# A complex-decay linear attention with two MLP layers: state factor written in one piece, its small transfers asked for where X and Y are formed, prologue and step pieces in a new order

## The chip, the cores and the metric

The kernel runs on one core of a Trainium2 chip. A time is the device time of one execution in microseconds (us), and the metric is the median over executions. The engines are PE (TensorE, matmuls, with PEld for its weight loads), DVE (VectorE), ACT (ScalarE), POOL (GpSimd) and SP (SyncE), which in this kernel asks for every transfer.

## The reference

Three parts follow one another. A linear attention with a complex decay per token and channel runs over 4 batches, 8 heads, 768 tokens and a head size of 48; its output, as 3072 tokens of 384 values, goes through two MLP layers with 2048 inner channels, the first with h cos(h), the second with ELU.

```python
mag = np.sqrt(a_re * a_re + a_im * a_im)
scale = np.minimum(mag, 0.999) / (mag + 1e-06)
a_re_n, a_im_n = (a_re * scale, a_im * scale)
for t in range(S):
    ar, ai = (a_re_n[:, :, t, :, None], a_im_n[:, :, t, :, None])
    new_re = ar * S_re - ai * S_im
    new_im = ar * S_im + ai * S_re
    kv = np.einsum('bhd,bhe->bhde', k[:, :, t], v[:, :, t])
    S_re, S_im = (new_re + kv, new_im)
    y[:, :, t] = np.einsum('bhd,bhde->bhe', q[:, :, t], S_re)
...
h = x @ w_in                                   # layer 1
g = h * np.cos(h)
x = g @ w_out
h = x @ w_in                                   # layer 2
g = np.where(h > 0.0, h, np.exp(np.minimum(h, 0.0)) - 1.0)
return g @ w_out
```

## The kernel before

**Attention.** The 768 tokens of a batch are cut into 6 chunks of 128. A step is one chunk c of one batch b; there are 24, in the order (0,0), (0,1), (0,2), (0,3), (1,0) and so on, so the same batch comes again four steps later. A step loads arai (a_re and a_im side by side), qk and v; forms the logarithm L of the decay's size and its angle th (`a1_pre`, `a1_ln`, `a1_lam`, `a1_th`); sums both over the chunk with a matmul by a triangle (`p_tl`, `p_tf`, L245, L247); and gets E and En, the exponentials of plus and minus the summed logarithm (`a2_exp`, ACT L262, L263), and the phase r (`a2_ph`, L279, L280), whose sine and cosine are cs (`a2_trig`, L291, L292). `a2_mag` (L299) multiplies E into q and En into k. `a2_xy` (L306) forms X from q and Y from k, each 128x768. `b_tr` (PE L314) transposes X and Y in two groups of four heads, `b_ev` evacuates the results as XT (ACT L323) and YT (L325), `b_sc` (PE L332) multiplies them to scores and masks these as AT (DVE L335), `b_y` (L357, L366) forms the outputs, and `b_ds` (PE L376, DVE L382 or L384) updates the state S of the batch by Y, v and the factor R. `x_split` (ACT L408, DVE L409) writes a step's output as two parts, xh and xl, of which the MLP takes three products for exactness. For steps 0 to 2 all these tiles lie in `scr`, memory that the weights take over later.

**What goes through DRAM.** Two rows of a step are wanted in another shape or by another step. R is E's last row, 384 values, wanted as 96x8 (twice the same 48x8): `a2_exp` writes it to r_d (L267) and fetches it twice (L270). The last row of r is the phase that the batch carries on: `a2_ph` writes it to f_d (L282), and four steps later `a1_carry` reads it into a row of the tile w (L237), which DVE adds to th (L228).

**MLP.** A block is three steps, 384 tokens. A unit is 128 of the 2048 inner channels for one block in one layer: nine matmuls into `work` (L504), a chain on ACT, DVE and POOL (for layer 1 ACT L558, DVE L559, ACT L575, DVE L576, then gh on ACT L175 and gl on POOL L176), and nine matmuls into `acc` (L610). Layer 1 runs eight units of block 0, eight of block 1, the other eight of each, then blocks 2 to 7 with 16 units each; layer 2 follows. Weights come as 64-bit floats in 16 tiles a layer: a load `raw` (L451), a decode `dec` on DVE and ACT (L466 or L469, L470, L471, L473), and a split into two parts (DVE L487 or ACT L489, then L491). Those of layer 2 are decoded during layer 1, written to w2f and read back.

**What sets the order.** The string PRO lists the prologue: tokens as `exp:1` are the part of that name for that step, and R, D and P the next weight's load, decode and split. From there on the list SLOT cuts each step into eight pieces, and a rule (`goal`) deals the pieces out between the MLP units so that a block's three steps are done before its units. J2 and J2E say how many blocks before the end of layer 1 the second layer's decodes begin and over how long they spread, WS the spread of splits. A scheduler then orders PE, DVE, POOL and SP by priorities; ACT keeps the order in which the code is written. YTA is the number of steps whose YT is evacuated on ACT, YG the number whose Y is formed on DVE and not POOL, ED the number of layer-1 weights whose first decode and split operations run on DVE and not ACT. Each engine runs its instructions in order, and SP waits at each transfer for what that transfer needs.

Of the kernel before, what the change touches and what calls it, by code (L numbers as in the profile page):

```python
# [11 lines left out]
F32 = mybir.dt.float32  # L12
# [22 lines left out]
YTA, RHP, CARP = 0, 0, 0  # L35
NDF = 24
MG, YG = 5, 3
KEEP = (1,)
J2, J2E = 4, 4
# [6 lines left out]
PRO = ('Q:2 L:1 L:0 V:1 L:2 V:0 R Q:0 R pre:1 Q:1 pre:0 ln:0 D pre:2 ln:1 ln:2 lam:0 lam:1 lam:2 tl:0 tl:1 tl:2 exp:0 exp:1 th:0 th:2 P L:3 exp:2 R mag:1 R tf:0 th:1 ph:0 tf:1 ph:1 mag:0 trig:0 xy:0 D tr0:0 tf:2 trig:1 tr1:0 ph:2 ev0:0 ds:0 ev1:0 xy:1 sc0:0 tr0:1 sc1:0 y0:0 tr1:1 trig:2 mag:2 y1:0 ev0:1 xy:2 xs:0 sc0:1 ev1:1 V:2 sc1:1 y0:1 y1:1 tr0:2 tr1:2 ds:1 ev0:2 ev1:2 D D sc1:2 pre:3 P sc0:2 xs:1 y0:2 ln:3 lam:3 y1:2 ds:2 xs:2 D th:3 P tf:3')  # L46
SLOT = ['xs:-1 pre:2', 'tl:1 tf:1 exp:1 ph:1 tr0 ev0 ln:2', 'tr1 sc0 y0 lam:2 ev1 trig:1', 'sl:2 L:3 sc1 mag:1',
        'ca:2', '', 'th:2', 'Q:2 sp:2 y1 xy:1 ds V:2']
NRAW, NDEC, NL, NTH = 3, 2, 1, 1
FA, NXB, ED, P0 = 8, 3, 5, 1  # L50
WS = 18
# [6 lines left out]
def tile_kernel(ctx, tc, q, k, v, a_re, a_im, w_in, w_out, w2_in, w2_out, ari, qk, vp, w1p, w2p, out):  # L58
# [23 lines left out]
    r_d = dram.tile([NS, D, H], F32, name="r_d")  # L82
# [173 lines left out]
    def a2_exp(i):  # L256
        s = st[i]
        c, b = steps[i]
        E = buf(i, "E")
        En = buf(i, "En")  # L260
        table(LN_SET)
        nc.scalar.activation(out=E, in_=s["Lp"][:, 0:HD], func=AF.Exp, scale=0.5)  # L262
        nc.scalar.activation(out=En, in_=s["Lp"][:, 0:HD], func=AF.Exp, scale=-0.5)  # L263
        s["E"], s["En"] = E, En
        if c < NCH - 1:
            R = ap.tile([D2, H], F32, name="R", bufs=2)
            nc.sync.dma_start(out=r_d[i:i + 1].rearrange("o d h -> o h d"),  # L267
                              in_=E[P - 1:P, :].rearrange("p (h d) -> p h d", h=H))
            for x in range(2):
                nc.sync.dma_start(out=R[x * D:(x + 1) * D, :], in_=r_d[i])  # L270
            s["R"] = R

    def a2_ph(i):
# [7 lines left out]
        if c < NCH - 1:  # L281
            nc.sync.dma_start(out=f_d[i:i + 1, :], in_=r[P - 1:P, :])  # L282
# [18 lines left out]
    def a2_xy(i):  # L301
        s = st[i]
        for nm, m, eng in (("X", "q", nc.vector), ("Y", "k", nc.vector if i < YG else nc.gpsimd)):
# [24 lines left out]
    def b_sc(i, g):  # L328
        s = st[i]
        ps = work()  # L330
# [38 lines left out]
    def b_ds(i):  # L369
        s = st[i]  # L370
        c, b = steps[i]
        if c == NCH - 1:
            return
        ps = work()
# [549 lines left out]
```

## Time and profile before

| | us |
|---|---|
| median of 3 executions | 1122.48 (1118.74 to 1123.85) |
| profiled execution | 1120.67 |
| its span | 1119.0 (1.7 lie outside) |
| PE busy in the span | 1048.4 (94%) |
| DVE busy | 636.9 (57%) |
| ACT busy | 744.4 (67%) |
| POOL busy | 493.6 (44%) |

The profile of one execution lists for each engine how long it worked; for a stretch, how much of it; for a group of equal operations, how many there were and how long one took; and the chain of waits, which is followed back from the last instruction of a stretch to what released each one. PE is idle for 70.6 us of the span in all. Of those, 26.8 lie before 60 us, 12.3 in 60 to 90, 8.7 in 90 to 150 and 6.9 in 150 to 240. The granted clock of PE is 1.00 at full speed (2.4 GHz) and 0.50 at half.

### The profile page before, as it was taken

The page shows a single profiled execution, that of the slowest core. Times are in us where ns is not written, and L with a number is a line of the kernel's source. Part 1 is how long each engine was busy: PE and PEld are TensorE (multiplying, and loading weights), DVE is VectorE, ACT ScalarE, POOL GpSimd, SP SyncE. Part 2 cuts the span into 40 slices and gives each one's busy share as a digit, 9 for nine tenths or more (in the row PEclk, how much of TensorE's full clock was granted, in tenths as well). Part 3 has the DMA queues.
Part 4 walks back from the last instruction along what each step waited for, and adds up shares of the span by engine and source line. Part 5 has one row for each costly group of instructions (what it writes and reads, how often), then busy time and mean ns, then how long its engine had stood idle before and what let it go on. Part 6 is the DMA issues. An engine that isn't in the chain of part 4 may idle for free.

```text
span 1119.0 us, 19085 instructions
## 1 busy us (share of the span) xinstructions
PE 1048.4 (94%) x7202; PEld 985.3 (88%) x7202; DVE 636.9 (57%) x1076; ACT 744.4 (67%) x1452; POOL 493.6 (44%) x422
## 2 busy tenths in 40 slices
PE   2877798999999999989999999999999999999997
PEld 0655686899999989989998799989999999999997
DVE  6885789855565646766876455554333333333332
ACT  6466677774776756766876356776666666666664
POOL 1023545454554534644754136783434343443432
PEclk9996899999999989989999999999999999999999
DMA  7744723321131351253443154541000010100000
GB/s 203 117 93 112 114 94 106 94 66 45 49 48 51 48 129 60 82 169 129 149 145 122 55 165 156 184 146 52 22 22 22 23 43 1 43 1 22 1 22 25
DMA packets 45397, 90.33 MB, mean 81 GB/s; under 512 B 14025, under 2 KB 24817, under 8 KB 45297
## 3 DMA queue, kind: packets, MB, share of 16 engines
q1 hardware_dynamic: 45296, 89.04, 28.7%
q8 instruction: 58, 0.95, 0.4%
q14 instruction: 43, 0.34, 0.1%
HBM read 72.05 MB, written 16.97 MB: 80 GB/s over the span
## 4 chain that ended last, share of the span: by engine, by line
PE 75%; ACT 8%; DVE 7%; DMA 4%; issue 3%; POOL 2%; SPq 0%; POOLq 0%; DVEq 0%; ACTq 0%
PE work L504 33%; PE acc L610 24%; PE work L610 6%; PE work L314 3%; ACT L94 3%; PE work L357 2%; PE work L332 2%; PE work L366 2%; DMA w<-f_d 1%; PE work L376 1%; DVE dec L471 1%; DVE AT L335 1%; DMA r_d<-E 1%; ACT XT L323 1%; PE work L245 1%
## 5 line engine op out<-in xcount | busy, mean ns | idle before, releaser
L504 PE MATMUL work<-xh,wt 128*128 128x384 f32 x1536 | 446.8, 346 | 4.7 <-POOL wt L491 2.3
L176 POOL TENSOR_TENSOR gl<-t,gh 128x384 fp32r<-128x384 f32 x256 | 277.6, 1086 | 375.5 <-ACT gh L175 147.2
L504 PEld LDWEIGHTS work<-xh,wt 128*128 128x128 f32 x1536 | 282.7, 191 | 15.2 <-issue 6.5
L504 PE MATMUL work<-xl,wt 128*128 128x384 f32 x768 | 223.5, 339 | 0.1
L610 PE MATMUL acc<-gh,wt 128*128 128x384 f32 x768 | 194.7, 346 | 1.5 <-ACT gh L175 1.1
L175 ACT CAST gh<-t 128x384 fp32r<-128x384 f32 x256 | 130.0, 508 | 98.0 <-PE acc L610 68.1
L565 DVE SCALAR_TENSOR_TENSOR t<-e,t 128x384 f32<-128x384 f32 x128 | 75.6, 591 | 204.9 <-ACT t L564 145.9
L610 PE MATMUL acc<-wt,gh 128*128 128x384 f32 x512 | 158.0, 334 | 0.0
L504 PEld LDWEIGHTS work<-xl,wt 128*128 128x128 f32 x768 | 142.0, 190 | 1.4 <-issue 1.0
L610 PEld LDWEIGHTS acc<-gh,wt 128*128 128x128 f32 x768 | 136.4, 190 | 7.2 <-ACT gh L175 3.3
L558 ACT ACTIVATE t<-work 128x384 int32<-128x384 f32 x128 | 61.7, 482 | 67.3 <-PE work L504 58.3
L610 PE MATMUL acc<-gl,wt 128*128 128x384 f32 x384 | 102.9, 338 | 2.0 <-POOL gl L176 1.8
L576 DVE TENSOR_TENSOR t<-work,t 128x384 f32<-128x384 f32 x128 | 70.6, 552 | 57.4 <-ACT t L575 57.2
L610 PEld LDWEIGHTS acc<-wt,gh 128*128 128x128 f32 x512 | 95.0, 188 | 0.0
L562 ACT ACTIVATE t<-work 128x384 f32<-128x384 f32 x128 | 62.8, 490 | 41.2 <-PE work L504 31.4
L559 DVE SCALAR_TENSOR_TENSOR t<-t,work 128x384 f32<-128x384 int32 x128 | 69.8, 546 | 30.8 <-ACT t L558 29.9
L306 POOL TENSOR_TENSOR Y<-cs,qk 128x768 f32<-128x768 f32 x21 | 51.2, 2440 | 78.6 <-ACT cs L292 35.9
L610 PE MATMUL work<-wt,gh 128*128 128x384 f32 x256 | 85.5, 334 | 0.0
L575 ACT ACTIVATE t<-t,hpi 128x384 f32<-128x384 f32 x128 | 78.9, 617 | 3.6 <-DVE t L559 3.5
L610 PE MATMUL acc<-wt,gl 128*128 128x384 f32 x256 | 76.2, 334 | 0.0
L578 DVE SCALAR_TENSOR_TENSOR t<-work,t 128x384 f32<-128x384 f32 x128 | 71.3, 557 | 4.3
L610 PEld LDWEIGHTS acc<-gl,wt 128*128 128x128 f32 x384 | 69.1, 188 | 4.3 <-POOL gl L176 3.6
(135 smaller groups left out, 1697.9 us busy)
## 6 DMA issues: line engine op xcount, KB each, us to landing
raw<-in_w1p_dram SPq DMA_DIRECT2D x16, 768.0 KB
raw<-in_w2p_dram SPq DMA_DIRECT2D x16, 768.0 KB
chk<-in_ari_dram SPq DMA_DIRECT2D x24, 384.0 KB
arai<-in_ari_dram SPq DMA_DIRECT2D x21, 384.0 KB
qk<-in_qk_dram SPq DMA_DIRECT2D x21, 384.0 KB
v<-in_vp_dram SPq DMA_DIRECT2D x24, 256.0 KB
w2f<-dec SPq DMA_DIRECT2D x16, 384.0 KB
raw<-w2f SPq DMA_DIRECT2D x16, 384.0 KB
```

Source lines behind the costliest of these rows:

```text
L175: nc.scalar.copy(out=hi, in_=x)
L176: nc.gpsimd.tensor_tensor(out=lo, in0=x, in1=hi.bitcast(F32), op=ALU.subtract)
L306: eng.tensor_tensor(out=t, in0=s["cs"], in1=mm.to_broadcast([P, H, 2, D]), op=ALU.mult)
L504: nc.tensor.matmul(out=out_ps, lhsT=a, rhs=b_, start=m == 0, stop=m == n - 1)
L558: nc.scalar.activation(out=ki, in_=h, func=AF.Copy, scale=1.0 / TWO_PI, bias=0.25)
L559: nc.vector.scalar_tensor_tensor(out=t, in0=ki, scalar=-TWO_PI, in1=h, op0=ALU.mult, op1=ALU.add)
L562: nc.scalar.activation(out=t, in_=h, func=AF.Relu, scale=-1.0)
L565: nc.vector.scalar_tensor_tensor(out=t, in0=e, scalar=1.0, in1=t, op0=ALU.add, op1=ALU.mult)
L575: nc.scalar.activation(out=t, in_=t, func=AF.Sin, bias=hpi)
L576: nc.vector.tensor_tensor(out=t, in0=h, in1=t, op=ALU.mult)
L578: nc.vector.scalar_tensor_tensor(out=t, in0=h, scalar=0.0, in1=t, op0=ALU.max, op1=ALU.add)
L610: nc.tensor.matmul(out=o, lhsT=a, rhs=b_, start=(l, j, ff) in first and x == 0, stop=(l, j, ff) in last and x == 2)
```

## The change

- r_d holds [step, head, channel] and not [step, channel, head]. The write of E's last row becomes one contiguous row of 384 values; each of the two fetches into the 48x8 halves of R now picks single values.
- The two writes (r_d and f_d) move from `a2_exp` and `a2_ph` into a function `send`, called at the start of `a2_xy`. The fetch moves into `fetch`, called at the first scores of a step (`b_sc`) or, if that has not been, in `b_ds`.
- YT of steps 0 to 3 is evacuated on ACT (YTA 0 to 4); Y of steps 3 to 8 is formed on DVE (YG 3 to 9); the sixth layer-1 weight's first decode operation and cast move to DVE (ED 5 to 6); WS goes from 18 to 17.
- The second layer's sixteen decodes lie in 30 units of blocks 5 and 6 (J2 5, J2E 2), before in 44 of blocks 4 to 6.
- PRO lists the prologue in a new order, and SLOT deals the parts of a step to the eight pieces in another way.

```diff
-YTA, RHP, CARP = 0, 0, 0
+YTA, RHP, CARP = 4, 0, 0
...
-MG, YG = 5, 3
+MG, YG = 5, 9
...
-J2, J2E = 4, 4
+J2, J2E = 5, 2
...
-PRO = ('Q:2 L:1 L:0 V:1 L:2 V:0 R Q:0 R pre:1 Q:1 pre:0 ln:0 D pre:2 ln:1 ln:2 lam:0 lam:1 lam:2 tl:0 tl:1 tl:2 exp:0 exp:1 th:0 th:2 P L:3 exp:2 R mag:1 R tf:0 th:1 ph:0 tf:1 ph:1 mag:0 trig:0 xy:0 D tr0:0 tf:2 trig:1 tr1:0 ph:2 ev0:0 ds:0 ev1:0 xy:1 sc0:0 tr0:1 sc1:0 y0:0 tr1:1 trig:2 mag:2 y1:0 ev0:1 xy:2 xs:0 sc0:1 ev1:1 V:2 sc1:1 y0:1 y1:1 tr0:2 tr1:2 ds:1 ev0:2 ev1:2 D D sc1:2 pre:3 P sc0:2 xs:1 y0:2 ln:3 lam:3 y1:2 ds:2 xs:2 D th:3 P tf:3')
+PRO = ('L:1 L:0 L:2 pre:1 pre:0 pre:2 R V:0 ln:2 D ln:0 lam:2 Q:2 V:1 lam:0 tl:0 tl:2 Q:0 ln:1 exp:0 lam:1 tl:1 th:1 Q:1 th:0 th:2 exp:2 exp:1 mag:0 P tf:0 R mag:1 ph:0 tf:2 tf:1 ph:1 L:3 trig:0 xy:0 trig:1 tr0:0 tr1:0 ev0:0 ph:2 sc0:0 ev1:0 xy:1 R sc1:0 trig:2 D tr0:1 y0:0 mag:2 ds:0 ev0:1 y1:0 sc0:1 pre:3 xs:0 xy:2 tr1:1 V:2 tr0:2 R y0:1 ev1:1 tr1:2 sc1:1 D ev0:2 y1:1 sc0:2 ev1:2 D xs:1 sc1:2 ds:1 y0:2 ln:3 ds:2 th:3 y1:2 P P D xs:2')
-SLOT = ['xs:-1 pre:2', 'tl:1 tf:1 exp:1 ph:1 tr0 ev0 ln:2', 'tr1 sc0 y0 lam:2 ev1 trig:1', 'sl:2 L:3 sc1 mag:1',
-        'ca:2', '', 'th:2', 'Q:2 sp:2 y1 xy:1 ds V:2']
+SLOT = ['xs:-1', 'tl:1 tf:1 pre:2 exp:1 ph:1 tr0 ev0 tr1 ln:2 ev1', 'lam:2', 'sc0',
+        'trig:1 sl:2', 'ca:2', 'mag:1 th:2 sc1 y0', 'xy:1 y1 L:3 ds sp:2 V:2 Q:2']
...
-FA, NXB, ED, P0 = 8, 3, 5, 1
-WS = 18
+FA, NXB, ED, P0 = 8, 3, 6, 1
+WS = 17
...
-    r_d = dram.tile([NS, D, H], F32, name="r_d")
+    r_d = dram.tile([NS, H, D], F32, name="r_d")
...
             R = ap.tile([D2, H], F32, name="R", bufs=2)
-            nc.sync.dma_start(out=r_d[i:i + 1].rearrange("o d h -> o h d"),
-                              in_=E[P - 1:P, :].rearrange("p (h d) -> p h d", h=H))
-            for x in range(2):
-                nc.sync.dma_start(out=R[x * D:(x + 1) * D, :], in_=r_d[i])
             s["R"] = R
+
+    def send(i):
+        s = st[i]
+        if steps[i][0] == NCH - 1 or "sent" in s:
+            return
+        s["sent"] = True
+        nc.sync.dma_start(out=r_d[i:i + 1].rearrange("o h d -> o (h d)"), in_=s["E"][P - 1:P, :])
+        nc.sync.dma_start(out=f_d[i:i + 1, :], in_=s["r"][P - 1:P, :])
+
+    def fetch(i):
+        s = st[i]
+        if steps[i][0] == NCH - 1 or "got" in s:
+            return
+        s["got"] = True
+        for x in range(2):
+            nc.sync.dma_start(out=s["R"][x * D:(x + 1) * D, :], in_=r_d[i].rearrange("h d -> d h"))
...
-        if c < NCH - 1:
-            nc.sync.dma_start(out=f_d[i:i + 1, :], in_=r[P - 1:P, :])
         s["r"] = r
...
     def a2_xy(i):
         s = st[i]
+        send(i)
...
     def b_sc(i, g):
         s = st[i]
+        fetch(i)
...
     def b_ds(i):
...
             return
+        fetch(i)
```

The new lines shift the code by 9 to 13 lines; L504 of before is L517 of after, L610 is L623, L306 is L317, L325 is L336, L382 is L395, L409 is L422, L466 is L479.

Three places show what moves. The first is SP around the transfers of step 3 (E, r, R) and those that steps 4 and 5 wait for: w is step 4's carry, arai is the load of step 5, qk that of step 5. Before:

```order
L451 DMA raw_602<-in_w1p_dram 128x1536
L267 DMA r_d_79<-E_622 8x48x1
L451 DMA raw_684<-in_w1p_dram 128x1536
L270 DMA R_627<-r_d_79 48x8 x2
L282 DMA f_d_80<-r_631 1x384
L153 DMA arai_668<-in_ari_dram 128x768
L237 DMA w_617<-f_d_80 1x384
L153 DMA qk_694<-in_qk_dram 128x768
```

After:

```order
L464 DMA raw_678<-in_w1p_dram 128x1536
L274 DMA r_d_79<-E_622 1x384
L275 DMA f_d_80<-r_628 1x384
L237 DMA w_619<-f_d_80 1x384
L153 DMA arai_694<-in_ari_dram 128x768
L283 DMA R_627<-r_d_79 48x8x1 x2
L153 DMA qk_697<-in_qk_dram 128x768
```

The fetch of R has moved from ahead of the carry and arai to behind both.

The second is DVE in the prologue, from the Y of one step to the score mask of the next. scr are the tiles of steps 0 to 2, tri is the mask. Before:

```order
L306 TENSOR_TENSOR scr_122<-scr_121 128x768
L325 COPY YT_272<-work_247 96x512
L471 SCALAR_TENSOR_TENSOR dec_430<-raw_152,dec_430 128x768
L280 SCALAR_TENSOR_TENSOR scr_125<-scr_125,work_252 128x384
L325 COPY YT_286<-work_262 96x512
L165 TENSOR_SCALAR scr_124<-scr_125 128x8x48
L335 TENSOR_TENSOR AT_295<-work_290,tri_88 128x512
L473 SCALAR_TENSOR_TENSOR dec_430<-raw_152,dec_430 128x768
L325 COPY YT_348<-work_302 96x512
L335 TENSOR_TENSOR AT_312<-work_307,tri_88 128x512
L306 TENSOR_TENSOR scr_123<-scr_124 128x768
```

After:

```order
L317 TENSOR_TENSOR scr_122<-scr_121 128x768
L483 TENSOR_SCALAR dec_405<-dec_405 128x768
L500 CAST wt_501<-dec_286 128x2x384
L292 SCALAR_TENSOR_TENSOR scr_125<-scr_125,work_212 128x384
L484 SCALAR_TENSOR_TENSOR dec_405<-raw_151,dec_405 128x768
L165 TENSOR_SCALAR scr_124<-scr_125 128x8x48
L347 TENSOR_TENSOR AT_264<-work_259,tri_88 128x512
L347 TENSOR_TENSOR AT_281<-work_276,tri_88 128x512
L317 TENSOR_TENSOR scr_123<-scr_124 128x768
```

The copies to YT are gone from DVE, and a later decode stands between the same operations.

The third is POOL from the first MLP units on, where gl is the MLP's second part, L the decay's size and Y the operation of steps 3 to 5. Before:

```order
L176 TENSOR_TENSOR gl_580<-t_544,gh_579 128x384
L189 TENSOR_TENSOR L_615<-L_615,w_617 128x384
L306 TENSOR_TENSOR Y_698<-cs_644,qk_612 128x768
L176 TENSOR_TENSOR gl_660<-t_563,gh_659 128x384
L189 TENSOR_TENSOR L_701<-L_701,w_703 128x384
L306 TENSOR_TENSOR Y_845<-cs_772,qk_694 128x768
L176 TENSOR_TENSOR gl_788<-t_585,gh_787 128x384
L189 TENSOR_TENSOR L_862<-L_862,w_864 128x384
```

After:

```order
L176 TENSOR_TENSOR gl_578<-t_541,gh_577 128x384
L189 TENSOR_TENSOR L_617<-L_617,w_619 128x384
L176 TENSOR_TENSOR gl_651<-t_560,gh_650 128x384
L189 TENSOR_TENSOR L_703<-L_703,w_705 128x384
L176 TENSOR_TENSOR gl_765<-t_583,gh_764 128x384
L189 TENSOR_TENSOR L_864<-L_864,w_866 128x384
```

The two Y have left POOL for DVE.

## Rows read from the trace of the kernel before

**Rows 1.** Busy us (instructions) by engine, then clock, DMA share, GB/s

```profile
60.00:90.00 30.00, 17.69 (x79) 14.52 (x79) 22.28 (x36) 17.27 (x32) 7.59 (x6) 0.86 0.51 120
90.00:150.00 60.00, 51.34 (x412) 43.13 (x411) 43.31 (x70) 44.54 (x81) 30.67 (x21) 0.81 0.49 94
150.00:240.00 90.00, 83.13 (x653) 75.41 (x651) 74.08 (x110) 65.62 (x125) 44.85 (x35) 0.98 0.34 101
480.00:500.00 20.00, 16.91 (x93) 16.35 (x92) 15.79 (x27) 15.28 (x28) 8.44 (x8) 0.83 0.44 135
520.00:580.00 60.00, 59.79 (x479) 56.40 (x478) 47.95 (x76) 49.29 (x94) 35.37 (x28) 1.00 0.40 130
```

**Rows 2.** The same for DVE alone, in the prologue

```profile
10.00:58.60 48.60, 42.19 (x71) 0.96 0.69 127
```

**Rows 3.** Chain of waits, 0 to 12: start, us, what

```profile
3.62 7.82 DMA raw<-in_w1p_dram
```

**Rows 4.** Single operations of DVE and PE: start, us, what

```profile
10.29 0.56 DVE L203 TENSOR_TENSOR scr<-scr 128x384 f32<-128x384 f32 x1 [8.29 <-ACT scr L200]
...
60.19 0.63 PE L504 MATMUL work<-xh,wt 128*128 128x384 f32 x1
```

**Rows 5.** Groups before 60: busy, mean ns, idle before

```profile
L306 DVE TENSOR_TENSOR scr<-scr 128x768 f32<-128x768 f32 x6 | 5.4, 947 | 0.0
L325 DVE COPY YT<-work 96x512 f32<-96x512 f32 x6 | 4.1, 682 | 2.1 <-PE work L314 2.1
...
L471 DVE SCALAR_TENSOR_TENSOR dec<-raw,dec 128x768 int32<-128x768 int32 x4 | 3.8, 945 | 0.0
...
L473 DVE SCALAR_TENSOR_TENSOR dec<-raw,dec 128x768 int32<-128x768 int32 x3 | 2.8, 949 | 0.0
...
L466 DVE TENSOR_SCALAR dec<-raw 128x768 f32<-128x768 f32 x4 | 2.2, 552 | 0.1
L470 DVE TENSOR_SCALAR dec<-dec 128x768 int32<-128x768 int32 x4 | 2.2, 549 | 0.0
L382 DVE TENSOR_TENSOR S<-work,R 96x384 f32<-96x384 f32 x3 | 1.7, 554 | 1.4 <-PE work L376 1.4
```

**Rows 6.** Chain of waits, 72 to 90

```profile
74.16 10.32 DMA r_d<-E
...
85.71 2.98 DMA arai<-in_ari_dram
...
89.32 0.98 PE work L245
```

**Rows 7.** Single operations of SP, DVE and ACT

```profile
33.62 0.77 SPq L270 DMA_DIRECT2D R<-r_d  x2
...
77.88 0.55 DVE L206 SCALAR_TENSOR_TENSOR th<-arai 128x384 f32<-128x384 f32 x1
...
81.68 0.82 ACT L489 CAST wt<-dec 128x768 fp32r<-128x768 f32 x1
...
88.63 0.55 DVE L228 TENSOR_TENSOR th<-th,w 1x384 f32<-1x384 f32 x1 [4.59 <-DMA w<-f_d]
```

**Rows 8.** Packets read in 74 to 77.5

```profile
DMA packets 416, 0.15 MB, mean 43 GB/s; under 512 B 392, under 2 KB 392, under 8 KB 416
```

**Rows 9.** Chain of waits, 118 to 136

```profile
120.81 2.38 DMA w<-f_d
...
134.90 2.58 POOL Y L306
```

**Rows 10.** Groups of the whole run

```profile
L504 PE MATMUL work<-xh,wt 128*128 128x384 f32 x1536 | 446.8, 346 | 4.7 <-POOL wt L491 2.3 <-DVE YT L325 1.3 <-DVE AT L335 1.1
...
L306 POOL TENSOR_TENSOR Y<-cs,qk 128x768 f32<-128x768 f32 x21 | 51.2, 2440 | 78.6 <-ACT cs L292 35.9 <-DVE L L211 26.8 <-issue 5.1
```

**Rows 11.** Chains of waits, 392 to 402 and 474 to 482

```profile
393.77 6.04 DMA w<-f_d
...
475.26 4.33 DMA w<-f_d
```

## The prediction

> **What bounds the kernel now.** I read the busy time by stage first, then the chain of waits where TensorE (PE) idles, then the single operations there. PE is the bound wherever it is full: from 520 to 580 us it works 59.79 of 60 [rows 1], and there a saving on another engine buys nothing. It is not full at the front: in 60–90 it works 17.69 of 30, in 90–150 51.34 of 60 at a granted clock of 0.81, in 150–240 83.13 of 90 [rows 1]. The reader is to see there three different limits.
>
> First, the stretch before the first MLP matmul, at 60.19 [rows 4]. VectorE (DVE) gets its first operation of the decay chain at 10.29, after 8.29 of idling [rows 4], and from 10.00 to 58.60, where the third xl (the MLP's input) ends, it is busy 42.19 of 48.60 [rows 2]: the prologue is DVE-bound with about 6.1 us of holes (48.3 from 10.3 on, less 42.2).
>
> Second, a stall in 60–90. The chain of waits has the 8x48 write of the state factor from 74.16 for 10.32 us, then the load of arai at 85.71 that lands in 2.98, then the cumulative-sum matmul on PE at 89.32 [rows 6]. SP, which asks for every transfer, stood in front of the fetch until the write had landed, and arai and the carry (w<-f_d) stood behind it; the carry's reader on DVE came at 88.63 after waiting 4.59 [rows 7]. It is no shortage of bandwidth: 392 of the 416 packets that were read from 74 to 77.5 are under 512 bytes, and the mean is 43 GB/s [rows 8]; the write's pieces had left by then, and it landed seven us later.
>
> Third, 150–240, where DVE is busy 74.08 of 90 [rows 1] and PE's holes are small.
>
> **The change, part by part.**
>
> *T1, the prologue: −6.* What DVE does before the third xl: six YT copies (steps 0 to 2) go to ScalarE (ACT), 6 x 0.682 = −4.1; in come one of each of the decode's operations L466, L471 and L473 and one more state write L382, 0.552 + 0.945 + 0.949 + 0.554 = +3.0 [rows 5]; and the first decode's 0.552 + 0.549 + 0.945 = 2.05 [rows 5] now stand before the decay chain in DVE's order, in the 8.29 that it idles, because their weight, now asked for as the seventh transfer at 3.62 and landing 7.82 later [rows 3], is asked for as the fourth. Left after 10.3: 42.2 − 4.1 + 3.0 − 2.05 = 39.05. With the same 6.1 of holes the third xl ends at 55.4 (gain 3), with none at 49.4 (gain 9); I take 6, since holes come from chains through ACT and PE that the new order loosens in part. ACT, which takes the copies, is not the fuller engine here. The matmuls on step 3's th and the ACT work ahead of them, which stood between the third xl and the first MLP matmul, now come after four MLP units, which protects the gain.
>
> *T2, the stall: −6.3.* The write becomes one row and is asked for where X and Y are formed; the fetch moves behind it to the scores. In SP's order of step 3 the carry and arai now stand ahead of the fetch, so nothing makes them wait for the write. arai then waits for its buffer's last reader, the operation L206 at 77.88 [rows 7], so it can be asked for at 78.4 and lands 2.98 later at 81.4, rather than at 85.71 + 2.98. PE's matmul behind it, at 89.32, moves up by up to 7.3. I take one less: ACT is in a weight cast from 81.68 for 0.82 [rows 7] when arai lands. Bounds −3 (next comes the weight decode, on DVE) and −7.
>
> *The row write and the fetch by themselves.* No row shows a one-row write of E, but the carry, of the same 384 values in a row, is read back in 2.38 [rows 9] in the best case and 6.04 in a crowded stretch [rows 11], so 2 to 6 us off every path is my price. The fetch turns from two transfers of 48 rows of 8 values into two of 384 single values. Nearest rows: arai's 2.98 below, the old write's 10.32 above [rows 6]. I take 5, nearer the lower: in the old write the pieces had gone out by 77.5 [rows 8] and the seven us after that were a wait for the landing of a write to DRAM; arai, read from DRAM right behind it, shows no such wait. R is needed only at the state update, which now stands some 45 MLP matmuls behind the first scores in a usual step (0.346 each [rows 10], some 15 us), so 5 is hidden. The Trainium skill speaks against this edit: "DMA: Bandwidth & Descriptors", section "Rules for kernel authors", holds that a strided last dimension makes one descriptor an element and wants such transfers rearranged. The change moves that form from the write to the fetch and doubles its elements; by that rule the fetch would cost at least the old write, which is the first rival below. The trace only shows the form on the write.
>
> *T3, the rest of 90–150: −4.* The next carry's 2.38 stands on the chain at 120.81 [rows 9] and ACT waits behind its reader; this goes when the phase is sent a piece earlier: −2.4. Y of steps 3 to 8 moves from GpSimd (2.44 each, 2.58 on the chain at 134.90 [rows 9, 10]) to DVE, where the same operation takes 0.947 [rows 5]: −1.6 where it is on the chain. Bounds −10 (the clock comes back from 0.81 as well) and +5 (DVE, 43.31 of 60, gets some three more operations of 0.947, and the old holes return elsewhere).
>
> *T4, 150–240: 0.* DVE has 74.08 of 90 and gets three more Y operations, 2.8 us, of a kind that took 2.44 each on GpSimd, where X and the scores of the next step had to wait for it. I set the one against the other. Bounds −4 and +4, an operation's length and a half at either price.
>
> *T5, after 240: −3.* Two holes of the carry remain there, 6.04 at 393.77 and 4.33 at 475.26 [rows 11]; in the slice around the second PE works 16.91 of 20 at a clock of 0.83 [rows 1]. Idle is 3.1 there and less at the first; sent earlier most of it goes: −3 to −7 with the clock. Against it the sixteen second-layer decodes fall into 30 units and not 44: at 2.44 of DVE for one [rows 5] that is 1.30 a unit rather than 0.89, and DVE in 520–580 goes from 47.95 to some 52 of 60 [rows 1], still below PE: 0 to +4. Bounds −7 and +4.
>
> Sum: −6 − 6.3 − 4 + 0 − 3 = −19.3 against the profiled execution's 1120.67 gives 1101.4; the median of the runs shown is 1.8 higher. I say **1102**. What this measurement can tell from no change is about 0.5%, 5.6 us.
>
> **The rivals.**
>
> *A, the fetch is as dear as the old write, piece for piece.* Then each fetch of 768 pieces takes 2 x 10.32 = 20.6 us. The place is the prologue: the first fetch is asked for at about 33.6, as in the kernel before [rows 7], three follow one another in the queue, and the state updates of steps 0 to 2 all stand ahead of the third xl on DVE now. That gives 33.6 + 61.9 + 1.1 (an update and an xl) = 96.6 for the third xl in place of the 52.6 that T1 gives (58.6 − 6): 44 us late, the stall of T2 swallowed either way: 1101.4 + 44 = 1145. With p for one fetch it decides from 33.6 + 3p + 1.1 = 58.6 + 13.3 on (T2 to T5 being the 13.3), p = 12.4, where the whole gain is eaten; slower by 0.5% from p = 14.3. For it: the skill's rule and the doubled count. Against it: the 77.5 at which the write's pieces were out [rows 8].
>
> *A half, a fetch of 10.3.* 33.6 + 31.0 + 1.1 = 65.7, 13 late: 1114.
>
> *B, the gain is handed to DVE.* An earlier start only brings more steps sooner to the stage in which DVE is the limit (74.08 of 90 [rows 1]): the loop's steps are dealt out by units, so a stretch that begins 12 us earlier still has the same DVE work. If T3 is void and half of T1 + T2 goes, 6.2, and nothing of T5 stays: 1120.67 − 6.2 = 1114; if T5 stays, 1111. For it: DVE's busy share rises by the Y operations. Against it: PE has only 6.9 of idle there, which it would have to double.
>
> *C, the denser decode hurts.* +4 in T5 in place of −3: 1108, inside my own range.
>
> *D, more is won.* T1 at 9, T3 at −10, T5 at −7: 1120.67 − 9 − 6.3 − 10 − 7 = 1088. The low clock in 90–150 is the lever: PE works 51.34 at 0.81 there [rows 1], and at 1.00 the same work would be some 10 us less.
>
> *E, the sends do not move.* If the row write's landing is still what SP waits for ahead of arai, T2 and the waits of T3 and T5 stay, and T1 alone remains: 1115. Against it is SP's order in step 3. Elsewhere SP's wait for the old write was hidden, so that it goes is worth no more than the places named.
>
> **How the numbers follow.** Forecast with C (1092 to 1109): 0.54. B 0.15, A half 0.09, E 0.04 (these three 1109 to 1120), A 0.09, D 0.09 (1085 to 1092). The range 1087 to 1118 leaves out A, the lower half of D and the upper end of B and E, some 0.17. Faster by over 0.5%, that is below 1115: 0.54 + 0.09 + 0.12 + 0.06 + 0.01 = 0.82; slower: A, 0.09; within 0.5%: 0.09.
>
> **What would show it.** T1: the first MLP matmul at 53 to 55, the third xl before it. T2: no wait on SP for r_d longer than some 3 us, the carry's reader of step 4 on DVE without its 4.59. Fetch: SP asks for R and the state update on DVE does not wait for it; if A holds, DVE stands before L395 in 33–97. T3: 90–150 with more than 51.34 of PE and a clock above 0.81. T5: no hole at 394 and 475, DVE at about 52 of 60 where the second layer is decoded. Wrong would make me: DVE at over 80 of 90 after the first MLP units, a R<-r_d in the chain of waits, or a stage in which POOL or ACT now ends the chain.

## The result

The changed kernel takes 1090.31 us (median of 3 executions, 1087.97 to 1090.90) against 1122.48 before: a ratio of 0.9715, with a 95% interval of 0.9672 to 0.9758. It is faster, by 32 us where 20 were forecast; the range of 1087 to 1118 holds it. The profiled execution has a span of 1086.3 against 1119.0.

Where the time went can be read off PE's own order. Each unit of the MLP begins with nine matmuls of the first product, so the (9n + 1)th of these, counted in the trace, marks how far the kernel is; units of one stretch interleave, which blurs a mark by a few us. In the table are the starts of such matmuls in us, in the profiled executions; "row write alone" and the others are experiments of the next section.

| unit n | before | changed | difference | list alone | row write alone | old form in the changed | list and places | four edits |
|---|---|---|---|---|---|---|---|---|
| 0 | 60.2 | 49.2 | −11.0 | 57.8 | 60.5 | 49.8 | 49.9 | 49.7 |
| 4 | 69.9 | 58.4 | −11.5 | 72.8 | 70.2 | 59.0 | 63.7 | 58.5 |
| 6 | 109.9 | 87.0 | −22.9 | 111.9 | 103.1 | 96.8 | 102.0 | 90.7 |
| 8 | 144.4 | 119.0 | −25.4 | 146.2 | 135.7 | 131.7 | 136.4 | 122.9 |
| 32 | 251.6 | 226.5 | −25.1 | 252.7 | 240.8 | 239.7 | 245.0 | 228.8 |
| 64 | 411.2 | 377.8 | −33.4 | 412.9 | 394.4 | 392.0 | 398.7 | 382.5 |
| 80 | 493.7 | 453.5 | −40.2 | 494.7 | 471.0 | 468.8 | 481.2 | 459.1 |
| 128 (layer 2) | 700.8 | 667.3 | −33.5 | 701.8 | 678.1 | 681.1 | 688.3 | 666.2 |
| 255 (last) | 1100.9 | 1067.7 | −33.2 | 1102.8 | 1079.6 | 1082.9 | 1089.5 | 1065.7 |

The changed kernel, profiled a second time (run 12), has the same marks within 0.9 us, but for unit 8, which came 2.4 earlier; differences of that size between two columns mean little.

So 11.0 are won ahead of the MLP, 14.4 more up to unit 8, nothing from there to unit 32, 8.1 from there to the end, and nothing in layer 2. The first rows of the profile after answer to [rows 1]: busy time by stage, with the columns given there.

```profile
60.00:90.00 30.00, 23.52 (x162) 18.89 (x161) 28.59 (x48) 28.93 (x54) 8.82 (x7) 0.94 0.41 116
90.00:150.00 60.00, 53.11 (x474) 48.36 (x473) 51.66 (x79) 44.86 (x83) 31.26 (x21) 0.91 0.39 123
150.00:240.00 90.00, 85.29 (x609) 78.05 (x609) 60.10 (x101) 63.44 (x123) 41.29 (x36) 1.00 0.24 68
480.00:500.00 20.00, 20.00 (x151) 19.25 (x144) 12.18 (x22) 13.62 (x26) 6.13 (x6) 0.86 0.34 96
520.00:580.00 60.00, 57.80 (x422) 52.23 (x422) 51.63 (x73) 42.59 (x82) 35.79 (x25) 0.94 0.51 171
```

PE in 60–90 works 23.52 and not 17.69, but DVE is now busy 28.59 of 30 there: the stall has gone and DVE is what is left. From 90 to 150 the clock is 0.91 and not 0.81. The holes of the carry [rows 11] are gone. PE is full in 480–500, but at a clock of 0.86, and from 520 to 580, where the second layer's decodes stand closer, DVE has 51.63 (the forecast said some 52) and PE has lost 2. Just ahead of the first stretch and within the second stands a wait of PE that the kernel before does not have, for a score mask that DVE forms late (in brackets the wait, in us, and what ended it):

```profile
479.22 0.66 PE L369 MATMUL work<-AT,v 128*32 128x128 f32 x8 [2.61 <-DVE AT L347]
...
559.02 0.43 PE L369 MATMUL work<-AT,v 128*32 128x128 f32 x8 [1.80 <-DVE AT L347]
```

In the chain of waits that leads to the first of them, two decode operations stand on DVE ahead of the mask, at 474.64 for 1.33 and at 477.23 for 0.87. Because everything lies some 25 to 40 us earlier, a stretch after does not hold quite the work of the same stretch before.

The prologue, in answer to [rows 2 to 4]: DVE's busy time from 10 us to the end of the third xl, and single operations of DVE and PE at its start and its end.

```profile
10.00:49.80 39.80, 39.04 (x69) 0.91 0.49 159
```

```profile
8.88 0.56 DVE L479 TENSOR_SCALAR dec<-raw 128x768 f32<-128x768 f32 x1 [6.88 <-DMA raw<-in_w1p_dram]
...
10.95 0.55 DVE L203 TENSOR_TENSOR scr<-scr 128x384 f32<-128x384 f32 x1
...
49.18 2.35 PE L517 MATMUL work<-xh,wt 128*128 128x384 f32 x12 [1.24 <-ACT xh L421]
...
49.23 0.55 DVE L422 TENSOR_TENSOR xl<-work,xh 128x384 fp32r<-128x384 f32 x1
```

DVE is busy 39.04 of 39.80: hardly a hole is left, before it was 42.19 of 48.60. The first decode starts at 8.88 in DVE's former idle time, and PE starts on xh at 49.18, before the third xl (49.23, done at 49.78) and before any matmul on th.

The stall of [rows 6, 7] is read in SP's transfers around step 3 of the changed kernel and in the chain of waits there:

```profile
61.93 0.25 SPq L274 DMA_DIRECT2D r_d<-E  x1
63.04 0.25 SPq L275 DMA_DIRECT2D f_d<-r  x1
66.00 0.21 SPq L237 DMA_DIRECT2D w<-f_d  x1
66.46 0.36 SPq L153 DMA_DIRECT2D arai<-in_ari_dram  x1
66.87 0.93 SPq L283 DMA_DIRECT2D R<-r_d  x2
...
70.47 4.28 DMA qk<-in_qk_dram
...
78.24 3.25 DMA arai<-in_ari_dram
```

The row write is asked for at 61.93, the carry at 66.00, arai at 66.46 and the fetch at 66.87, and none of them waits for a write. What the chain still shows of transfers are 4.28 and 3.25 us of loads that DVE's own pace released late. SP's waits for r_d from step 3 on (us in total, times, the longest) are, in the kernel before:

```profile
SPq L270 <- DMA r_d<-E: 111.5, 17, 9.1
```

and in the changed kernel:

```profile
SPq L283 <- DMA r_d<-E: 0.2, 1, 0.2
```

### The profile page after: what moved, and what is told of

It is laid out like the page before. It is cut to its first block, busy times and chain, and to the rows that moved or that the text cites. A ratio compares the mean times of both kernels' runs of the same rounds, so it can differ in the third digit from the quotient of the medians.

```text
span 1086.3 us, 19099 instructions
## 1 busy us (share of the span) xinstructions
PE 1029.3 (95%) x7202; PEld 978.0 (90%) x7202; DVE 639.4 (59%) x1076; ACT 744.9 (69%) x1458; POOL 486.8 (45%) x416
## 4 chain that ended last, share of the span: by engine, by line
PE 74%; DVE 10%; ACT 5%; issue 4%; DMA 4%; POOL 2%; SPq 0%; DVEq 0%; POOLq 0%; ACTq 0%
PE work L517 31%; PE acc L623 25%; PE work L623 6%; PE work L325 3%; DMA chk<-in_ari_dram 2%; PE work L344 2%; PE work L378 2%; PE work L369 2%; PE work L389 2%; POOL gl L176 1%; DVE t L589 1%; DVE dec L484 1%; DVE dec L486 1%; ACT L94 1%; POOL ltl L176 1%
## 5 line engine op out<-in xcount | busy, mean ns | idle before, releaser
L176 POOL TENSOR_TENSOR gl<-t,gh 128x384 fp32r<-128x384 f32 x256 | 281.7, 1103 | 429.7 <-ACT gh L175 199.4
L517 PE MATMUL work<-xh,wt 128*128 128x384 f32 x1536 | 444.2, 344 | 6.7 <-POOL wt L504 2.8
L517 PEld LDWEIGHTS work<-xh,wt 128*128 128x128 f32 x1536 | 277.8, 189 | 17.8 <-issue 7.3
L517 PE MATMUL work<-xl,wt 128*128 128x384 f32 x768 | 227.6, 341 | 0.1
L623 PE MATMUL acc<-gh,wt 128*128 128x384 f32 x768 | 199.6, 347 | 3.4 <-ACT gh L175 2.8
L623 PE MATMUL acc<-wt,gh 128*128 128x384 f32 x512 | 158.0, 334 | 0.0
L623 PEld LDWEIGHTS acc<-gh,wt 128*128 128x128 f32 x768 | 138.6, 191 | 8.5 <-ACT gh L175 3.6
L517 PEld LDWEIGHTS work<-xl,wt 128*128 128x128 f32 x768 | 140.9, 188 | 2.6 <-issue 1.8
L623 PE MATMUL acc<-gl,wt 128*128 128x384 f32 x384 | 105.0, 341 | 1.2 <-POOL gl L176 1.2
L623 PEld LDWEIGHTS acc<-wt,gh 128*128 128x128 f32 x512 | 94.9, 188 | 0.0
L623 PE MATMUL work<-wt,gh 128*128 128x384 f32 x256 | 85.5, 334 | 0.0
L623 PE MATMUL acc<-wt,gl 128*128 128x384 f32 x256 | 76.2, 334 | 0.0
L623 PEld LDWEIGHTS acc<-gl,wt 128*128 128x128 f32 x384 | 71.0, 191 | 1.8 <-POOL gl L176 1.8
L576 ACT ACTIVATE e<-t 128x384 f32<-128x384 f32 x128 | 67.4, 527 | 4.1
```

The lines of the kernel that those rows point to most:

```text
L176: nc.gpsimd.tensor_tensor(out=lo, in0=x, in1=hi.bitcast(F32), op=ALU.subtract)
L517: nc.tensor.matmul(out=out_ps, lhsT=a, rhs=b_, start=m == 0, stop=m == n - 1)
L576: nc.scalar.activation(out=e, in_=t, func=AF.Exp, scale=-1.0)
L623: nc.tensor.matmul(out=o, lhsT=a, rhs=b_, start=(l, j, ff) in first and x == 0, stop=(l, j, ff) in last and x == 2)
```

## The experiments

Each ratio is against runs of the kernel before that were taken beside it on the same chip.

**1. The prologue's list alone** (the kernel before with the new PRO).

```diff
-PRO = ('Q:2 L:1 L:0 V:1 L:2 V:0 R Q:0 ...
+PRO = ('L:1 L:0 L:2 pre:1 pre:0 pre:2 R V:0 ...
```

> The kernel before with the new prologue list alone. The changed kernel's first MLP matmul came at 49.2 rather than 60.2. Theory (the list makes these 11 us, and they are kept to the end, since the MLP's units can start with the weights already there): first MLP matmul at 49 to 51, total 1108 to 1113. Rival 1 (the YT copies moved to ACT make half of it): first MLP matmul at 53 to 56, total 1112 to 1117. Rival 2 (the stall behind the old write, or DVE in 150 to 240, takes it back): first matmul early, total 1117 to 1122.

Measured: 1122.58 against 1116.85, ratio 1.0037 (1.0011 to 1.0062). The list alone gains nothing; it loses a little. The first MLP matmul came at 57.8. Busy time of DVE from 30 to 50, in this kernel, and single operations of SP, ACT and DVE there:

```profile
30.00:50.00 20.00, 10.77 (x18) 0.78 0.33 99
...
27.16 1.42 SPq L267 DMA_DIRECT2D r_d<-scr  x2
...
35.86 2.87 SPq L270 DMA_DIRECT2D R<-r_d  x2
...
39.12 0.36 SPq L153 DMA_DIRECT2D arai<-in_ari_dram  x1
...
42.17 0.52 ACT L186 ACTIVATE L<-arai 128x384 f32<-128x384 f32 x1 [7.74 <-DMA arai<-in_ari_dram]
...
43.51 0.56 DVE L409 TENSOR_TENSOR xl<-work,xh 128x384 fp32r<-128x384 f32 x1 [6.96 <-ACT xh L408]
```

SP asks for two writes of the old form from 27.16 on, stands in front of the fetch until 35.86, and only then asks for step 3's arai, at 39.12. ACT, which keeps the written order, has waited 7.74 for arai at 42.17 and so comes late to xh; DVE, full up to 30, waits 6.96 behind that and works 10.77 of 20. None of the three cases written down was quite this: the early start never came about, because the old write already holds SP in the prologue.

**2. The form alone** (the kernel before with the one-row write and the single-value fetch, both where they were).

```diff
-    r_d = dram.tile([NS, D, H], F32, name="r_d")
+    r_d = dram.tile([NS, H, D], F32, name="r_d")
...
-            nc.sync.dma_start(out=r_d[i:i + 1].rearrange("o d h -> o h d"),
-                              in_=E[P - 1:P, :].rearrange("p (h d) -> p h d", h=H))
+            nc.sync.dma_start(out=r_d[i:i + 1].rearrange("o h d -> o (h d)"), in_=E[P - 1:P, :])
             for x in range(2):
-                nc.sync.dma_start(out=R[x * D:(x + 1) * D, :], in_=r_d[i])
+                nc.sync.dma_start(out=R[x * D:(x + 1) * D, :], in_=r_d[i].rearrange("h d -> d h"))
```

> The kernel before with the one-row write and the single-value fetch, both at their old places. Theory (the form of the write makes the stall at 74 to 89: it landed after 10.3 and now after 1 to 4, and SP stands in front of the fetch only that long): the cumulative-sum matmul after the stall some 6 earlier, total 1112 to 1116. Rival (the place makes it: SP still stands before the fetch, and arai and the carry behind it): 1119 to 1123. If the fetch of single values is dear, above 1125 and DVE waits for R before 60.

Measured: 1098.05 against 1116.85, ratio 0.9824 (0.9772 to 0.9875). This is more than the theory gave, and some six tenths of the whole gain by the ratios (1.8 of 2.9 per cent). SP's waits for r_d, and its transfers around one step, in this kernel:

```profile
SPq L269 <- DMA r_d<-E: 4.0, 5, 3.1
...
371.16 0.28 SPq L267 DMA_DIRECT2D r_d<-E  x1
...
373.50 0.89 SPq L269 DMA_DIRECT2D R<-r_d  x2
...
375.63 0.33 SPq L153 DMA_DIRECT2D arai<-in_ari_dram  x1
376.70 0.25 SPq L237 DMA_DIRECT2D w<-f_d  x1
```

The same step in the kernel before:

```profile
381.97 0.65 SPq L267 DMA_DIRECT2D r_d<-E  x1
...
391.28 0.79 SPq L270 DMA_DIRECT2D R<-r_d  x2
...
393.11 0.61 SPq L153 DMA_DIRECT2D arai<-in_ari_dram  x1
393.77 0.32 SPq L237 DMA_DIRECT2D w<-f_d  x1
```

From the write to the fetch SP needs 2.3 us now (371.16 to 373.50) and needed 9.3 (381.97 to 391.28); the carry comes 5.5 behind the write and not 11.8. The table above shows where that paid: 7.1 between units 4 and 6, where the stall was, 1.9 in the next two, 2.1 from there to unit 32, 5.9 between units 32 and 64 and 6.0 between 64 and 80, which are the two holes of [rows 11]. Before the first MLP matmul the form alone gives nothing (60.5), and DVE keeps its holes there. Its busy time in this kernel, beside the 42.19 of [rows 2]:

```profile
10.00:58.60 48.60, 41.85 (x71) 0.96 0.39 126
```

**3. The old form in the changed kernel** (the write of single values and the fetch of rows of 8, at the new places).

```diff
-    r_d = dram.tile([NS, H, D], F32, name="r_d")
+    r_d = dram.tile([NS, D, H], F32, name="r_d")
...
-        nc.sync.dma_start(out=r_d[i:i + 1].rearrange("o h d -> o (h d)"), in_=s["E"][P - 1:P, :])
+        nc.sync.dma_start(out=r_d[i:i + 1].rearrange("o d h -> o h d"),
+                          in_=s["E"][P - 1:P, :].rearrange("p (h d) -> p h d", h=H))
...
-            nc.sync.dma_start(out=s["R"][x * D:(x + 1) * D, :], in_=r_d[i].rearrange("h d -> d h"))
+            nc.sync.dma_start(out=s["R"][x * D:(x + 1) * D, :], in_=r_d[i])
```

> The changed kernel with the old write of 384 single values and the old fetch of rows of 8, at the new places. Theory (the form counts beside the places, because SP meets the fetch of the same step soon behind the write and stands there for up to 10 us, in the prologue too): total 1097 to 1106. Rival (the places alone do it, arai and the carry stand ahead of the fetch): 1089 to 1093, as the changed kernel.

Measured: 1102.50, ratio 0.9865 (0.9820 to 0.9909), in the theory's range. But the early start stays (49.8), where the theory had the prologue suffer too. What is lost is the stretch up to unit 8, where 2.3 are left of 14.4; the holes at 394 and 475 stay closed, with 13.0 won between units 32 and 80 (15.1 in the changed kernel). SP's waits for r_d in this kernel, the chain of waits from 62 to 97, and SP's transfers there:

```profile
SPq L284 <- DMA r_d<-E: 106.8, 17, 7.4
...
67.09 8.15 DMA arai<-in_ari_dram
...
78.09 9.25 DMA r_d<-E
...
62.56 0.67 SPq L274 DMA_DIRECT2D r_d<-E  x1
...
66.62 0.24 SPq L237 DMA_DIRECT2D w<-f_d  x1
67.09 0.35 SPq L153 DMA_DIRECT2D arai<-in_ari_dram  x1
73.07 0.77 SPq L284 DMA_DIRECT2D R<-r_d  x2
...
87.36 0.33 SPq L284 DMA_DIRECT2D R<-r_d  x1
88.19 0.35 SPq L153 DMA_DIRECT2D arai<-in_ari_dram  x1
88.67 0.23 SPq L237 DMA_DIRECT2D w<-f_d  x1
```

Three things are to be seen. The new places do not spare SP the wait: 106.8 us, against 111.5 before. In the next step the first half of the fetch (87.36) still stands ahead of arai (88.19) and the carry (88.67), behind the write of 78.09 that takes 9.25. And where arai was asked for ahead of the fetch, at 67.09, it landed 8.15 later, with the write asked for at 62.56 still under way. Behind a landed write the load of arai took 2.98 [rows 6], and the load asked for at the same place of the changed kernel, at 66.46 (above), landed 2.96 later, by the times at which the trace has its parts land. The weights of layer 1 show the same: in the kernel before, of the thirteen that are asked for after 20 us, the five asked for while an old write was under way landed after 11.1 to 11.8, the other eight after 4.0 to 6.1. So the old write delays SP and, while it lasts, also the transfers that are asked for behind it.

**4. The second layer's decodes spread as before** (in the changed kernel).

```diff
-J2, J2E = 5, 2
+J2, J2E = 4, 4
```

> The changed kernel with the second layer's decodes spread over 44 units of blocks 4 to 6 as before. In the changed kernel its lead over the kernel before falls from 40 us at the 80th unit to 33.5 at the 104th, where the sixteen decodes lie. Theory (the denser decode gives these 6 back): total 1083 to 1087. Rival (the wider spread takes as much from blocks 4 and 5, where attention steps run): 1089 to 1095.

Measured: 1084.90, in the theory's range, ratio 0.9708 (0.9665 to 0.9752), the changed kernel's own being 0.9715 (and 0.9738 in run 12): no difference that these runs can tell. In the trace unit 128 starts at 667.2 and not 667.3, and unit 80 at 458.6 and not 453.5: 5 us of the lead at unit 80 go with decodes put off (up to there DVE has run 54 operations of the decode in the changed kernel and 66 here), and the fall from 40 to 33.5 comes where they are made up. The closer decodes alone do not make that fall: with the old pieces (experiment 8) the lead is some 36 both at unit 80 and at unit 128.

**5. List and places together, old form** (the kernel before with the new PRO, `send` and `fetch`).

```diff
+PRO = ('L:1 L:0 L:2 pre:1 pre:0 pre:2 R V:0 ...
...
     def a2_xy(i):
         s = st[i]
+        send(i)
...
     def b_sc(i, g):
         s = st[i]
+        fetch(i)
```

> The kernel before with the new prologue list and the new places of the sends and the fetch, the write and fetch still in the old form, no other number changed. The new list alone brought the first MLP matmul only from 60.2 to 57.8, and DVE was busy 10.8 of 20 from 30 to 50, behind SP, which stood in front of the fetch for the old write. Theory (list and places together make the early start: SP no longer stands ahead of step 3's loads): first MLP matmul at 50 to 53, DVE above 18 of 20 in 30 to 50. Rival (it is the six YT copies on ACT): first MLP matmul at 54 to 58. Total by the first 1102 to 1112, by the second 1110 to 1120.

Measured: 1109.61 against 1117.66, ratio 0.9935 (0.9902 to 0.9969). The first MLP matmul came at 49.9, and DVE's busy time from 30 to 50 is, in this kernel:

```profile
30.00:50.00 20.00, 18.28 (x32) 0.95 0.49 129
```

18.28 where the list alone had 10.77. The early start needs the new list (the form alone gives 60.5) and SP free of the old write in the prologue (the list alone gives 57.8); it does not need the YT copies on ACT. At unit 4 (63.7), though, only 6.2 of the 10.3 are left, and from there to the end of the loop only the hole at 394 is added to that.

**6. YT of steps 0 to 3 on DVE again** (in the changed kernel).

```diff
-YTA, RHP, CARP = 4, 0, 0
+YTA, RHP, CARP = 0, 0, 0
```

> The changed kernel with the YT copies of steps 0 to 3 back on DVE (eight copies of 0.68, six of them ahead of the third xl). Theory (DVE is full up to there, so they are on the path): first MLP matmul 3 to 4 later, at 52.3 to 53.2, total 1092 to 1096. Rival (other work fills DVE's holes and ACT is freed): first MLP matmul at 49 to 51, total 1088 to 1092.

Measured: 1092.80, ratio 0.9780 (0.9744 to 0.9817). The first MLP matmul came at 49.9, as the rival said; but unit 4 came at 63.7, 5.3 after the changed kernel's, and the last at 1071.7, 4.0 after it. PE's matmuls in this kernel:

```profile
49.86 2.37 PE L517 MATMUL work<-xh,wt 128*128 128x384 f32 x12 [1.16 <-ACT xh L421]
...
58.27 0.76 PE L517 MATMUL work<-xh,wt 128*128 128x384 f32 x3 [0.45 <-DVE wt L500]
```

At 58.27 PE waits for a weight that DVE casts (L500). The copies are paid for in the decodes of the weights, which stand behind the prologue's own work on DVE, and not ahead of the first matmul. Unit 4 starts at 63.7 in both kernels with the early start and YT on DVE (experiments 5 and 6), and at 58.2 to 59.4 in all nine with YT on ACT. In the whole time the interval still overlaps the changed kernel's, so the size, some 4 us, rests on the traces.

**7. Y of steps 3 to 8 on POOL again** (in the changed kernel).

```diff
-MG, YG = 5, 9
+MG, YG = 5, 3
```

> The changed kernel with Y of steps 3 to 8 back on POOL. Theory of the prediction (POOL takes 2.4 and more for what DVE does in 0.95, and the chain waits for it): total 1092 to 1097, the loss in 60 to 150. Rival (DVE is the fullest engine in 60 to 90, 28.6 of 30, so 5.7 us taken from it come back): 1084 to 1088.

Measured: 1088.29, ratio 0.9714 (0.9679 to 0.9748): level with the changed kernel. Its profiled execution has the longer span (1091.2 against 1086.3, with 3.5 lost up to unit 8), which its other executions don't bear out; neither theory nor rival is shown.

**8. The old pieces of a step** (the changed kernel with the SLOT of before).

```diff
-SLOT = ['xs:-1', 'tl:1 tf:1 pre:2 exp:1 ph:1 tr0 ev0 tr1 ln:2 ev1', ...
+SLOT = ['xs:-1 pre:2', 'tl:1 tf:1 exp:1 ph:1 tr0 ev0 ln:2', ...
```

> The changed kernel with the old eight pieces of a step. The changed kernel gains 14 us between its first and its ninth MLP unit, the one-row write alone 9. Theory (the new pieces are worth the 5 us in between, by the transposes that stand together and early): total 1094 to 1099, the loss in 60 to 150. Rival (they come from the other edits): 1088 to 1092.

Measured: 1084.80, ratio 0.9683 (0.9652 to 0.9715). The theory fell: with the old pieces unit 8 starts 4.8 later (123.8), but unit 32 only 1.1 later (227.6), and layer 2 begins 2.1 earlier (665.2). So the lead of the new pieces in the first units does not last. It is not attention work put off: up to unit 8 PE has run 592 matmuls of the attention in the changed kernel and 584 here. Why it is lost between units 8 and 32 stays open.

**9 to 12.** Four kernels side by side on one chip. The ninth is the kernel before with four edits only:

```diff
-YTA, RHP, CARP = 0, 0, 0
+YTA, RHP, CARP = 4, 0, 0
...
+PRO = ('L:1 L:0 L:2 pre:1 pre:0 pre:2 R V:0 ...
...
+    r_d = dram.tile([NS, H, D], F32, name="r_d")
...
+        send(i)
...
+        fetch(i)
```

> The kernel before with four edits alone: the one-row write with the single-value fetch, the new places, the new prologue list, YT of steps 0 to 3 on ACT. Pieces of a step, Y on POOL, the second layer's decodes and the other numbers as before. Theory (these four carry the whole gain): first MLP matmul at 49 to 51, total within 4 of the changed kernel, 1085 to 1093. Rival (pieces, Y and decode numbers hold some of it together, though each alone showed nothing): 1096 to 1104.

The tenth is the same with the short write and its fetch where they were before:

```diff
-        send(i)
...
-        fetch(i)
```

> The same without the new places: one-row write, fetch, prologue list and YT on ACT, all transfers asked for at the old places. Theory (the places matter only as long as the write takes 8 to 10 us; one that lands in 1 to 4 holds SP up little): first MLP matmul at 49 to 52, total within 4 of the kernel with the four edits. Rival (SP in front of the fetch still keeps step 3's loads back): first MLP matmul at 53 or later, total 4 to 10 more.

The eleventh is the changed kernel with two edits taken back:

```diff
-J2, J2E = 5, 2
+J2, J2E = 4, 4
...
-SLOT = ['xs:-1', 'tl:1 tf:1 pre:2 exp:1 ph:1 tr0 ev0 tr1 ln:2 ev1', ...
+SLOT = ['xs:-1 pre:2', 'tl:1 tf:1 exp:1 ph:1 tr0 ev0 ln:2', ...
```

> The changed kernel with the old pieces of a step and the old spread of the second layer's decodes, each of which alone came out level or a little faster. If they add: 1080 to 1084. If the differences were chance: 1085 to 1091, as the changed kernel.

And the changed kernel again:

> The changed kernel as it is, beside the three others on one chip, so that they can be compared with it: 1086 to 1091.

| run | median | ratio to before (1117.49) | 95% interval | first MLP matmul |
|---|---|---|---|---|
| 9, four edits | 1087.85 | 0.9729 | 0.9693 to 0.9765 | 49.7 |
| 10, old places | 1087.95 | 0.9735 | 0.9697 to 0.9774 | 49.9 |
| 11, old pieces, old decodes | 1082.35 | 0.9672 | 0.9636 to 0.9707 | 50.4 |
| 12, the changed kernel | 1088.66 | 0.9738 | 0.9702 to 0.9774 | 49.0 |

Run 9 carries the whole gain, and run 10 shows that once the write is short the places are worth nothing; this is SP's wait in run 10, and the prologue's DVE in it:

```profile
SPq L269 <- DMA r_d<-E: 5.8, 7, 2.6
...
30.00:50.00 20.00, 18.79 (x32) 0.93 0.26 70
```

Three edits, then, carry the gain: the form of the write, the list, and YT on ACT, the last with a share that only the traces show (experiment 6). Run 11 is the fastest of all, by 6 us of the medians; its interval just meets the changed kernel's, and its profiled execution, with a span of 1085.5 against 1085.2, is not shorter. But seven of its eight executions lie below all six of run 12, and the two waits of PE shown above, for the masks at 479.22 and 559.02, are not in its trace. Such a pair, of 2.6 and 1.8 us, is in all five traces that have the new pieces and the closer decodes together (the changed kernel, run 12, experiments 3, 6 and 7) and in none of those that lack one of the two. From unit 32 to unit 128 run 11 wins 11.9 on the kernel before, the changed kernel 8.1, run 12 8.6. That run 11 beats the changed kernel is likely and not settled.

## Why the prediction was right, and where its steps were off

The direction, the places in time and the range held. The first and the last term were too small by 5 us each, and the cause of the second was put in the wrong edit. The time lies in the band of 1085 to 1092 to which the prediction gave a chance of 0.09.

**T1 (−6; measured −11.0).** The sum of DVE's work was right but for one decode operation of 0.55 that it left out (L470): with no holes it gave 49.4 for the third xl, and it ended at 49.78. The step that was off is the choice between "the same 6.1 of holes" and none: the middle was taken, and next to none was right. The reason that the prediction gave, chains through ACT and PE that the new order loosens, is borne out: 3.5 us of DVE's idle time before 60 us stand behind PE [rows 5], and such holes stay when the old write alone goes (experiment 2). What it did not see is a condition. With the old write at its old place the new list brings a hole of its own, 6.96 us behind SP (experiment 1), so the list pays only where SP is free. Of the other 2 us, some 1.6 are the matmuls on th and the ACT work ahead of them, which had stood between the third xl and the MLP and were named but not priced; 0.6 come because PE now starts on xh before the third xl is done. The 4.1 for the YT copies were about right in size and stand in another place: the first MLP matmul comes as early without them, and some 4 us are lost at unit 4, behind the weights (experiment 6).

**T2 (−6.3; 7.1 by the form alone).** The size was right, but by luck, since the working was not. It said that nothing makes arai and the carry wait once they stand ahead of the fetch. In experiment 3, with the old write, they do stand there in step 3, and arai took 8.15 instead of 2.96; in the next step half of the fetch stands ahead of them after all. The stretch from unit 4 to unit 6 lasted 37.8, against 40.0 before and 28.6 in the changed kernel. The form of the write removes the stall; its place and the fetch's do nothing once the form is changed (run 10). The row of packets [rows 8] pointed at this: with a weight of 768 KB asked for right behind the write, only 0.15 MB were read in 3.5 us, and it was read as a matter of the landing alone.

**T3 (−4) and T4 (0).** From unit 4 to unit 8 the changed kernel gained 13.9, of which T2 and T3 gave 10.3. DVE's waits for the carry at L228 (19.2 us in 7 places before) are gone, as forecast. The term for Y on DVE is not borne out: with Y back on POOL the time is level (run 7). The 3 to 4 us left over go with the new pieces and do not last (experiment 8), so they are no gain: runs 9 and 10, with the old pieces, won 10.1 and 10.5 between units 4 and 8, about the 10.3. From unit 8 to unit 32 nothing was won or lost, as T4 had it; what it gave as the limit there, DVE, fell from 74.08 to 60.10 of the same 90 us, because work had moved ahead of it: from 60 to 240 DVE works 139.7 before and 140.4 after.

**T5 (−3; measured −8.1).** The gain was sized by PE's idle time near each hole, 3 to 7 for both. Experiment 2 gives 5.9 and 6.0, that is 12. A hole cost the idle time and what PE then did at the low clock: before, PE worked 16.91 of 20 in 480–500 at a clock of 0.83 [rows 1], and with the row write alone the same stretch is

```profile
480.00:500.00 20.00, 20.00 (x174) 18.59 (x173) 13.54 (x20) 11.81 (x26) 11.78 (x9) 1.00 0.40 129
```

The row that was nearer to it stood in the argument, the waits of 6.04 and 4.33 [rows 11], which sum to 10.4. That sending earlier closes a hole, as T5 had it, is shown for the one at 394 (experiment 5, in the old form); the one at 475 closes in the old form only with the other edits as well (experiment 3, 13.0 between units 32 and 80). So neither hole needs the new form to close, and the worth of the form and that of the other edits are not to be added there. What is taken back, some 4 (12 less 8.1), lies at the bound that was given for the denser decode, but it takes the new pieces as well: with the old pieces the same decodes leave 11.7 from unit 32 to unit 128 (experiment 8), and with the new pieces and the old spread 10.5 are left (experiment 4).

**The rivals.** A (a fetch as dear as the old write) did not come: before the state update of the first steps DVE waits for PE 0.3 us and for R not at all. The groups on that line of the changed kernel:

```profile
L395 DVE TENSOR_TENSOR S<-work,R x4: 547/550/554, 38.3 to 82.4; 96x384 f32<-96x384 f32 x4
...
  PE work L389: 0.3, 1
```

From the request to the last landing that the trace has, a fetch takes 1.9 to 4.2 in the first 120 us, where 5 had been taken and 20.6 feared; the old fetch, with an eighth of the pieces, took 2.3 to 4.1 in the loop and up to 8.5 in the prologue, that one with an old write under way beside it. The Trainium skill's rule in "DMA: Bandwidth & Descriptors", section "Rules for kernel authors", against a strided last dimension paid for the write to DRAM: by the trace the 20 old writes landed after 7.6 to 13.4 us, those of a row after 1.1 to 3.8. For the read, which has the form of single values now, it shows no price. Whether the direction makes the difference is not settled, since by the trace an old write lands in 8 parts and a fetch in 16. B (the gain handed to DVE) showed in 60–90, where DVE is now at 28.59 of 30, and it did not take the gain back. C (the denser decode hurts) is what T5 gave back, together with the new pieces. E (the sends don't move) did not come, and run 10, with the row write at the old places, shows that its price was wrong: SP waits 5.8 us there in all and the gain is whole. D (1088) is what came nearest, with a chance of 0.09.

## What to carry to other kernels

A small transfer is judged by how long its landing keeps a queue, and not by its bytes: look in the chain of waits for a write after which the issuing engine stands, and change its form before its place. An edit can be worth nothing until another clears the way for it: the new list alone gained nothing, and brought the early start only where SP did not stand in front of the old write. So ask of each part of a change what else must hold for it to pay. A lead read in the middle of a run may be lost again; it counts where the last stage begins.

## What the hardware showed that was not expected

The same 384 values, picked singly, took 7.6 to 13.4 us to be written to DRAM (9.25 and 10.32 in the chains shown) and at most 4.2 to be read from it, while as one row they were written in 1.1 to 3.8. And transfers that were asked for while such a write was under way took longer, though they have nothing to do with its data: a load of 384 KB 8.15 against 2.96, loads of 768 KB 11.1 to 11.8 against 4.0 to 6.1. A crowded stretch can do the like without a write: the arai asked for at 393.11 in the kernel before landed after 8.6, with the last old write already landed.
